# Two normed tiles of a fused transformer block: transposed by DMA and TensorE in halves, instead of by TensorE alone

## The chip, the cores and the metric

The kernel runs on one core of one Trainium2 chip. A core has five engines that matter here, each with an instruction order of its own: TensorE (PE, with its weight loads as PEld), VectorE (DVE), ScalarE (ACT), GpSimd (POOL) and SyncE (SP), which in this kernel issues nearly all DMAs. They meet only at semaphores: an instruction waits until the data that it reads are written and the buffer that it writes is free. The metric is the device time of one execution in microseconds (us); lower is better.

## The reference

The input is x, 2048 rows of 512 bf16 values, with a conditioning vector c. Cut to what matters:

```python
mod = (silu(c) @ w_mod).reshape(1, 6, 1, -1)         # sa, ca, ga, sb, cb, gb
h = layernorm(x) * (1 + ca) + sa                      # first norm
q, k, v = split(h @ wqkv)                             # 32 heads of 16
logits = q[s] . k[s - 2*w] / 4,  w = 0..7             # sliding, dilated window; masked below row 0
x = x + ga * ((softmax(logits) @ v) @ wo)
h = layernorm(x) * (1 + cb) + sb                      # second norm
x = x + gb * ((gelu(h @ w_gate) * (h @ w_up)) @ w_down)   # width 1792
```

Each row is normed twice. The normed rows then go into a product over the 512 columns, for which TensorE needs them with the columns on the partitions: each norm's output must be transposed.

## The kernel before, in words

**Tiling.** The 2048 rows are worked in 4 groups (sg 0 to 3) of 512 rows, each as 4 chunks (c4) of 128 rows, one row per partition. The 512 columns are 4 quarters (dt) of 128. LN1.1 means the first norm of group 1, LN2.0 the second norm of group 0, and so on.

**A norm.** For each chunk DVE takes the statistics (L430, L431; in some norms ACT does a chunk instead, L419); DVE adds the epsilon (L460, L465); GpSimd raises to the power -0.5 (`rs`, L471); DVE writes the normed chunk `xn` (L448, ops x0 to x3). The columns are then transposed, and at the same time or after it scaled by 1 + c and shifted by s, one quarter at a time (ops h0 to h3).

**Three ways to transpose.** `transp` (L475) and `transp_ev` (L514) hold two of them. By TensorE, for the norms in `BY_PE` (LN1.1 and LN2.0): two ops t0 and t1 of eight 128x128 transposes each, into PSUM (tile hTp, L484), then ACT evicts a quarter at a time with scale and shift (L527, 128x512). By DMA, for the norms of groups 1 to 3 otherwise: one transposing DMA on SP of all 16 blocks (L490), straight into the tile hT or h2, which ACT scales in place (L527), or GpSimd does for the norms in `H_POOL` (LN1.2; L525). LN1.0 has a way of its own by TensorE (`transp0`, `transp0_ev`, L509, L543, L545), which feeds the first products (L580).

**What uses them.** `qkv` (L588, products at L598) makes q (blk 0), k (blk 1) and v (blk 2) of a group, in four parts j; op qp.1.0.0 is the first product of group 1. Each takes four matmuls, one for each quarter. Loads for it are wqkv0 to wqkv2 (L223). `ffn_mm` (L826, products at L834) makes the gate and up products; g.0.0 is the first one of group 0.

**The attention** of a group: DVE multiplies q by the eight shifted k (`pq`, L659, op pq.sg.j), TensorE sums over a head with a 32-wide matrix of ones (`lp`, L673), DVE and ACT do the softmax (mx L690, z L696, e L701, s1 L706, ri L712, p L717). v goes to DRAM and back in shifted copies (`vst`, `V4`, L630, L639), the probabilities likewise (L745) or through TensorE, DVE multiplies them (`pv`, L766), TensorE sums (L780) and applies the output weights (`x1_mm`, L801), DVE adds the rest (L810).

**Order.** Every part is a generator ("thread") that yields `Op`s: engine, a cost, a function that issues the instructions, and what it waits for. `Issuer.run` (L94) takes the list `ORDER` (L19), a written-out list of thread numbers, and issues the next op of the thread named:

```python
for i in ORDER:
    op = nxt[i]
    assert all(name in self.done for name in op.after), (op.fire, op.after)
    ...
    op.fn()
```

So `ORDER` fixes the instruction order of every engine and of SP's DMA queue; `after`, `take` and `give` only state what must have been issued before. Nothing is reordered when the kernel runs.

Of the kernel before, what the change touches and what calls it, by code (L numbers as in the profile page):

```python
# [8 lines left out]
ACT = mybir.ActivationFunctionType  # L9
ALU = mybir.AluOpType  # L10
# [96 lines left out]
def kernel(  # L107
# [367 lines left out]
    def transp(key, dkey, dtag, ev):  # L475
        if ev in BY_PE:
            for dtp in range(2):
                def f(dtp=dtp):
                    hp = T("att", [P, CPS, 2, P], BF16, "hTp")
                    B[key, dtp] = hp  # L480
                    for c4 in range(CPS):
                        for dd in range(2):
                            dt = 2 * dtp + dd
                            nc.tensor.transpose(hp[:, c4, dd, :], B[key][:, c4, dt * P:(dt + 1) * P], ident[:])  # L484
                yield Op("PE", 0.445, f, after=[f"{ev}.x3", "ident"], take=[SL["att"]], give=[SL["xn"]] if dtp else [],
                         fire=f"{ev}.t{dtp}")
        else:
            def f():
                B[dkey] = T(dtag, [P, CPS, DT, P], BF16, dtag)
                nc.sync.dma_start_transpose(out=B[dkey][:].rearrange("p c d s -> p (c d) s"),  # L490
                                            in_=B[key][:].rearrange("p c d -> p (c d)"))
            yield Op("SP", 1.65, f, after=[f"{ev}.x3"], take=[SL[dtag]], give=[SL["xn"]], fire=f"{ev}.t", lat=1.0)
# [3 lines left out]
    BY_PE = ('LN1.1', 'LN2.0')  # L496
# [17 lines left out]
    def transp_ev(key, dkey, dtag, sc, bi, ev, dep):  # L514
        pe = ev in BY_PE
        for dtp in range(2):
            for dd in range(2):
                dt = 2 * dtp + dd

                def f(dt=dt, dtp=dtp, dd=dd):  # L520
                    if pe and dt == 0:
                        B[dkey] = T(dtag, [P, CPS, DT, P], BF16, dtag)
                    o = B[dkey][:, :, dt, :]
                    if ev in H_POOL:
                        nc.gpsimd.tensor_scalar(out=o, in0=o, scalar1=sc(dt), scalar2=bi(dt), op0=ALU.mult, op1=ALU.add)  # L525
# [26 lines left out]
    def ln1(sg):  # L552
        ev = f"LN1.{sg}"
        yield from norm(lambda: B["x", sg], lambda c4: [f"x0.{c4 // 2 * 2}"] if sg == 0 else [f"x{sg}"], ev,
                        PARTS0 if sg == 0 else ((0, 4),))
# [3 lines left out]
    def ln1_x(sg):  # L559
        yield from norm_x(("xn1", sg), lambda: B["x", sg], f"LN1.{sg}", PARTS0 if sg == 0 else ((0, 4),))  # L560

    def ln1_ev(sg):
        yield from transp_ev(("xn1", sg), ("hT", sg), "hT", lambda d: mod01[:, 4 + d:5 + d], lambda d: mod01[:, d:d + 1],
                             f"LN1.{sg}", ["mod01"])

# [22 lines left out]
    def qkv(sg):  # L588
        if sg == 0:
            yield from qkv_halves()  # L590
        for n, (blk, j) in enumerate(QKV if sg else QKV0):
# [10 lines left out]
            yield Op("PE", 0.865, f, after=[f"LN1.{sg}.h{d}" for d in (("0.1", "1.0", "3.1") if sg == 0 else (2, 3))] + [f"wqkv{blk}"], take=[SL["mm"]] + tk,  # L602
# [326 lines left out]
    for sg in range(NSG):  # L929
        for n, g in (("sa1", lambda q: norm_act(lambda: B["x", q], lambda c4: [f"x{q}"] if q else ["x0.2", "x0.0"], f"LN1.{q}")),  # L930
                     ("sa2", lambda q: norm_act(lambda: B["x", q], lambda c4: [f"x1.{q}.{c4}"], f"LN2.{q}")), ("ln1", ln1), ("ln1x", ln1_x), ("t1", lambda q: transp(("xn1", q), ("hT", q), "hT", f"LN1.{q}") if q else transp0(("xn1", 0), "LN1.0")), ("h1", lambda q: ln1_ev(q) if q else ln1_ev0(False)), ("qkv", qkv),
# [36 lines left out]
```

## Time and profile before

| What | Value |
|---|---|
| median of 3 runs | 237.67 us (237.32 to 238.6) |
| the profiled execution | 237.21 us |
| its span, first to last instruction | 235.0 us |
| granted TensorE clock in it | 1.0 |
| TensorE busy | 230.8 us |
| DVE busy | 170.1 us |
| ACT busy | 150.9 us |
| GpSimd busy | 17.9 us |

How to read it: the span is one execution as the hardware profiler recorded it; about 2 us lie outside it. Starts are in us from the start of the span. A row of the timeline has start, duration, engine, line, operation, output<-inputs, shapes and the count of instructions that it joins; matmuls overlap, so a row's duration is longer than the time it takes from the next. In brackets stands the idle time ahead of it and what ended that. The chain of work that ended last is followed back from the last instruction, at each step to what released it. Rows of DMA issues give the time from issue to landing as their last number.

### The profile page before, as it was taken

The numbers are of one execution on the slowest core, as the hardware profiler recorded it, in microseconds if no ns is written. First come the engines' busy times: TensorE is split into PE (matmuls) and PEld (weight loads), VectorE is DVE, ScalarE is ACT, GpSimd is POOL, SyncE is SP. The second block draws the span as 40 slices with busy tenths as digits, with TensorE's granted clock in tenths as the row PEclk, the third lists the DMA queues.
The fourth block names the chain that finished last, engine by engine and source line by source line (L and its number), as shares of the span: only waits on it lengthen the run. The fifth ranks groups of instructions, "written<-read, shape, count | busy, mean of one in ns | idle before, by whom it ended". The sixth has DMA issues, their size and how long they took to land.

```text
span 235.0 us, 3679 instructions
## 1 busy us (share of the span) xinstructions
PE 230.8 (98%) x1387; PEld 108.4 (46%) x1387; DVE 170.1 (72%) x238; ACT 150.9 (64%) x286; POOL 17.9 (8%) x43
## 2 busy tenths in 40 slices
PE   7999999999999999999999999999999999999995
PEld 2656454444644444444444444444444444444443
DVE  3899999999969999999899899279296211322222
ACT  4899997887996659937647862447636733367400
POOL 2612351000100000100000010000001000000000
PEclk9999999999999999999999999999999999999999
DMA  6998999999975859753100895320002210000011
GB/s 213 374 267 277 214 207 177 246 307 360 199 184 157 295 149 208 121 113 100 59 0 4 157 196 99 120 62 0 0 3 40 50 45 22 25 0 0 0 47 45
DMA packets 36265, 30.21 MB, mean 129 GB/s; under 512 B 14872, under 2 KB 34328, under 8 KB 36248
## 3 DMA queue, kind: packets, MB, share of 16 engines
q1 hardware_dynamic: 35968, 29.72, 50.7%
q8 instruction: 11, 0.18, 0.3%
q10 hardware_dynamic: 280, 0.26, 0.3%
q14 instruction: 6, 0.05, 0.1%
HBM read 22.37 MB, written 4.98 MB: 116 GB/s over the span
## 4 chain that ended last, share of the span: by engine, by line
PE 96%; ACT 2%; DVE 0%; issue 0%
PE u_ps L834 21%; PE g_ps L834 21%; PE y_ps L846 19%; PE qkv_ps L598 16%; PE x_ps L801 6%; PE LTp L673 3%; PE o_ps L780 3%; PE warm_ps L217 3%; PE y_ps L858 1%; PE hTp L484 1%; PE qkv_ps L580 1%; ACT hT L545 1%; ACT gl L419 1%; ACT LTp L701 0%; PE modT_ps L305 0%; PE modT_ps L348 0%
## 5 line engine op out<-in xcount | busy, mean ns | idle before, releaser
L834 PE MATMUL g_ps<-h,Wg 128*128 128x512 bf16 x224 | 57.5, 379 | 0.0
L834 PE MATMUL u_ps<-h,Wu 128*128 128x512 bf16 x224 | 57.5, 379 | 0.0
L868 ACT ACTIVATE gl<-g_ps 128x512 bf16<-128x512 f32 x56 | 33.5, 599 | 25.4 <-PE g_ps L834 22.1
L875 ACT CAST ub<-u_ps 128x512 bf16<-128x512 f32 x56 | 32.8, 586 | 21.4 <-PE u_ps L834 21.3
L846 PE MATMUL y_ps<-Wd,hht 128*128 128x512 bf16 x210 | 46.3, 379 | 0.0
L598 PE MATMUL qkv_ps<-hT,wqkv 128*128 128x512 bf16 x184 | 41.8, 380 | 0.1
L886 DVE TENSOR_TENSOR hht<-gl,ub 128x512 bf16<-128x512 bf16 x56 | 22.6, 420 | 25.2 <-ACT ub L875 23.2
L659 DVE TENSOR_TENSOR pq<-qT,kT 128x4096 bf16<-128x4096 bf16 x16 | 36.2, 2284 | 0.3 <-PE o_ps L780 0.2
L766 DVE TENSOR_TENSOR pv<-PT,V 128x4096 bf16<-128x4096 bf16 x16 | 35.9, 2283 | 0.0
L834 PEld LDWEIGHTS <-Wu 128*128 128x128 bf16 x224 | 21.6, 98 | 27.2 <-issue 1.9
L834 PEld LDWEIGHTS <-Wg 128*128 128x128 bf16 x224 | 21.6, 98 | 27.1 <-issue 1.7
L846 PEld LDWEIGHTS <-hht 128*128 128x128 bf16 x210 | 20.6, 98 | 24.8
L598 PEld LDWEIGHTS <-wqkv 128*128 128x128 bf16 x184 | 20.3, 114 | 19.6 <-issue 2.3
L893 DVE TENSOR_TENSOR ot<-y_ps,x 128x512 bf16<-128x512 f32 x15 | 10.3, 688 | 22.9 <-PE y_ps L846 22.9
L471 POOL TENSOR_TENSOR rstd<-rstd,neghalf 128x4 f32<-128x4 f32 (+1 forms) x9 | 8.9, 990 | 151.0 <-DVE rstd L460 81.3
L801 PE MATMUL x_ps<-woP,oT 128*128 128x512 bf16 x64 | 15.1, 379 | 0.0
L430 DVE BATCH_NORM_STATS2 st<-x 128x6 f32<-128x512 bf16 x18 | 12.3, 685 | 3.2 <-DMA x<-in_A_x_dram 2.9
L810 DVE TENSOR_TENSOR x<-x_ps,x 128x512 bf16<-128x512 f32 x16 | 10.8, 678 | 3.6 <-PE x_ps L801 3.4
L527 ACT ACTIVATE h<-h,modT,scl 128x512 bf16<-128x512 bf16 x12 | 8.8, 803 | 6.8 <-DMA h<-xn 6.8
L791 ACT CAST oT<-o_ps 128x512 bf16<-128x512 f32 x16 | 9.1, 590 | 3.5 <-PE o_ps L780 3.5
L620 ACT CAST kT<-qkv_ps 128x512 bf16<-128x512 f32 x16 | 9.6, 599 | 1.5 <-PE qkv_ps L598 1.4
L801 PEld LDWEIGHTS <-oT 128*128 128x128 bf16 x64 | 6.9, 109 | 7.1 <-issue 0.4
(84 smaller groups left out, 184.8 us busy)
## 6 DMA issues: line engine op xcount, KB each, us to landing
V<-vscr SPq DMA_DIRECT2D x12, 520.0 KB, 9.4
wm<-in_w_mod_dram SPq DMA_DIRECT2D x6, 512.0 KB, 5.9
vscr<-vT SPq DMA_DIRECT2D x4, 512.0 KB, 4.5
out_dram<-ot SPq DMA_DIRECT2D x15, 128.0 KB, 1.7
Wg<-in_B_w_gate_dram SPq DMA_DIRECT2D x1, 1792.0 KB
Wu<-in_B_w_up_dram SPq DMA_DIRECT2D x1, 1792.0 KB, 18.4
wqkv<-in_A_wqkv_dram SPq DMA_DIRECT2D x3, 512.0 KB, 8.5
x<-in_A_x_dram SPq DMA_DIRECT2D x3, 512.0 KB, 7.6
```

Source lines behind the costliest of these rows:

```text
L430: nc.vector.bn_stats(out=st[:], in_=src()[:, c4, :])
L598: nc.tensor.matmul(ps[:], lhsT=wqkv[blk][:, dt, j::4], rhs=B["hT", sg][:, :, dt, :], start=(dt == 0), stop=(dt == DT - 1))
L659: nc.vector.tensor_tensor(out=pq[:], in0=_ap(B["qT", sg][:, j, :], [[0, W], [1, SG]]), in1=_ap(kT[:, j, sg * SG + 2:sg * SG + 2 + SG], [[2 ...
L766: nc.vector.tensor_tensor(out=t[:], in0=_ap(B["PT", sg][:, 0, :], [[SG, 2], [0, 4], [1, SG]]), in1=_ap(v[:, 0, j, :], [[8, 2], [4 * (SG + ...
L801: nc.tensor.matmul(ps[:], lhsT=B["oT", sg][:, j, c4::CPS] if sg else B["oT", sg][:, j, c4 * P:(c4 + 1) * P], rhs=woP[:, j, :], start=(j == ...
L810: nc.vector.tensor_tensor(out=x[:, c4, :], in0=B["x1ps", sg, c4][:], in1=x[:, c4, :], op=ALU.add)
L834: nc.tensor.matmul(ps[:], lhsT=Wt[:, dt, ft * P:(ft + 1) * P], rhs=B["h2T", sg][:, :, dt, :], start=(dt == 0), stop=(dt == DT - 1))
L846: nc.tensor.matmul(ps[:], lhsT=B["hh", sg, ft][:, c4 * P:(c4 + 1) * P], rhs=B["Wd", ft // 4][:, ft % 4, :], start=(ft == 0), stop=(ft == F ...
L868: nc.scalar.activation(out=gl[:], in_=B["g", sg, ft][:], func=ACT.Gelu_apprx_tanh)
L875: nc.scalar.copy(out=ub[:], in_=B["u", sg, ft][:])
L886: nc.vector.tensor_tensor(out=hh[:], in0=B["gl", sg, ft][:], in1=B["ub", sg, ft][:], op=ALU.mult)
L893: nc.vector.tensor_tensor(out=ot[:], in0=B["y", sg, c4][:], in1=B["x", sg][:, c4, :], op=ALU.add)
```

## The change

For LN1.1 and LN2.0 the tile is transposed in two halves. `BY_PE` is emptied and a new `HALF` names the two norms.

- The first two chunks: as soon as x1 is written, one transposing DMA on SP moves their 8 blocks into the tile hT or h2. GpSimd scales and shifts them in place, a quarter at a time (ops hp0 to hp3, 128x256), in new threads.
- The last two chunks: one op t1 of 8 transposes on TensorE into PSUM, and four evictions of 128x256 on ACT (h0 to h3). These wait for the DMA too.
- The statistics of both norms are closed in two parts (`PARTS0`): two small steps on DVE and two powers on GpSimd (rs0, rs2) instead of one each.
- `qkv` of group 1 and `ffn_mm` of group 0 also wait for hp3.
- `ORDER` is a new list throughout.

In the new order, on SP: x1, x2, wqkv1, wqkv2, x3, wo0, LN1.1's transpose, wm2, wm3, the other wo blocks; and later V4.1.0, LN2.0's transpose, V4.1.1, V4.1.2 (before: x1, wqkv1, x2, and V4.1.0 to V4.1.2 in one piece). On GpSimd: rs0 and rs2 of LN1.1, hp0, rs0 of LN1.2, hp1, hp2, hp3; and rs0, rs2, hp0 to hp3 of LN2.0. On DVE around LN2.0: the last statistics, x0, x1, the softmax's z, x2, x3, s1, ri, p, then pq.2.0 and pq.2.1 in a row.

```diff
 ORDER = [
...
+        elif ev in HALF:
+            def f():
+                B[dkey] = T(dtag, [P, CPS, DT, P], BF16, dtag)
+                nc.sync.dma_start_transpose(out=B[dkey][:, 0:2].rearrange("p c d s -> p (c d) s"),
+                                            in_=B[key][:, 0:2].rearrange("p c d -> p (c d)"))
+            yield Op("SP", 1.65, f, after=[f"{ev}.x1"], take=[SL[dtag]], fire=f"{ev}.t", lat=0.5)
+
+            def f():
+                B[key, 0] = T("att", [P, DT, 2, P], BF16, "hTp")
+                for dt in range(DT):
+                    for c4 in range(2):
+                        nc.tensor.transpose(B[key, 0][:, dt, c4, :], B[key][:, 2 + c4, dt * P:(dt + 1) * P], ident[:])
+            yield Op("PE", 0.445, f, after=[f"{ev}.x3", "ident"], take=[SL["att"]], give=[SL["xn"]], fire=f"{ev}.t1")
...
-    BY_PE = ('LN1.1', 'LN2.0')
+    BY_PE = ()
+
+    HALF = ('LN1.1', 'LN2.0')
+
+    HALF_POOL = ('LN1.1', 'LN2.0')
...
     def transp_ev(key, dkey, dtag, sc, bi, ev, dep):
         pe = ev in BY_PE
+        if ev in HALF:
+            for dt in range(DT):
+                def f(dt=dt):
+                    nc.scalar.activation(out=B[dkey][:, 2:4, dt, :], in_=B[key, 0][:, dt, :, :], func=ACT.Identity,
+                                         scale=sc(dt), bias=bi(dt))
+                yield Op("ACT", 0.455, f, after=[f"{ev}.t1", f"{ev}.t"] + dep, give=[SL["att"]] if dt == DT - 1 else [],
+                         fire=f"{ev}.h{dt}")
+            return
...
+    def half_ev(dkey, sc, bi, ev, dep):
+        for dt in range(DT):
+            def f(dt=dt):
+                o = B[dkey][:, 0:2, dt, :]
+                if ev in HALF_POOL:
+                    nc.gpsimd.tensor_scalar(out=o, in0=o, scalar1=sc(dt), scalar2=bi(dt), op0=ALU.mult, op1=ALU.add)
...
+            yield Op("POOL" if ev in HALF_POOL else "ACT", 0.44 if ev in HALF_POOL else 0.47, f, after=[f"{ev}.t"] + dep,
+                     fire=f"{ev}.hp{dt}")
...
-        yield from norm(lambda: B["x", sg], lambda c4: [f"x1.{sg}.{c4}"], ev)
+        yield from norm(lambda: B["x", sg], lambda c4: [f"x1.{sg}.{c4}"], ev, PARTS0 if ev in HALF else ((0, 4),))
...
-        h2 = [f"LN2.{sg}.h3"]
+        h2 = [f"LN2.{sg}.h3"] + ([f"LN2.{sg}.hp3"] if f"LN2.{sg}" in HALF else [])
```

More of the change, by code (lines that the diff above doesn't have):

```diff
@@ L531, in transp_ev @@
                          give=[SL["att"]] if pe and dd == 1 else [], fire=f"{ev}.h{dt}")
+    def half_ev(dkey, sc, bi, ev, dep):
[4 more added lines that the diff above has]
+                    nc.gpsimd.tensor_scalar(out=o, in0=o, scalar1=sc(dt), scalar2=bi(dt), op0=ALU.mult, op1=ALU.add)
+                else:
+                    nc.scalar.activation(out=o, in_=o, func=ACT.Identity, scale=sc(dt), bias=bi(dt))
+            yield Op("POOL" if ev in HALF_POOL else "ACT", 0.44 if ev in HALF_POOL else 0.47, f, after=[f"{ev}.t"] + dep,
+                     fire=f"{ev}.hp{dt}")
     def transp0_ev(key, dkey, sc, bi, ev, dep, eng):
@@ L554, in ln1 @@
         yield from norm(lambda: B["x", sg], lambda c4: [f"x0.{c4 // 2 * 2}"] if sg == 0 else [f"x{sg}"], ev,
-                        PARTS0 if sg == 0 else ((0, 4),))
+                        PARTS0 if sg == 0 or f"LN1.{sg}" in HALF else ((0, 4),))
     PARTS0 = ((0, 2), (2, 4))
     def ln1_x(sg):
-        yield from norm_x(("xn1", sg), lambda: B["x", sg], f"LN1.{sg}", PARTS0 if sg == 0 else ((0, 4),))
+        yield from norm_x(("xn1", sg), lambda: B["x", sg], f"LN1.{sg}", PARTS0 if sg == 0 or f"LN1.{sg}" in HALF else ((0, 4),))
     def ln1_ev(sg):
@@ L564, in ln1_ev, with ln1_evh @@
                              f"LN1.{sg}", ["mod01"])
+    def ln1_evh(sg):
+        yield from half_ev(("hT", sg), lambda d: mod01[:, 4 + d:5 + d], lambda d: mod01[:, d:d + 1], f"LN1.{sg}", ["mod01"])
     def ln1_ev0(onv):
@@ L601, in qkv @@
             tk = {0: [SL["q"]], 1: [], 2: [SL["vs"]]}[blk] if j == 0 else []
-            yield Op("PE", 0.865, f, after=[f"LN1.{sg}.h{d}" for d in (("0.1", "1.0", "3.1") if sg == 0 else (2, 3))] + [f"wqkv{blk}"], take=[SL["mm"]] + tk,
+            yield Op("PE", 0.865, f, after=[f"LN1.{sg}.h{d}" for d in (("0.1", "1.0", "3.1") if sg == 0 else (2, 3))] + ([f"LN1.{sg}.hp3"] if f"LN1.{sg}" in HALF else []) + [f"wqkv{blk}"], take=[SL["mm"]] + tk,
                      give=[SL["hT"]] if last else [], fire=f"qp.{sg}.{blk}.{j}")
@@ L814, in ln2 @@
         ev = f"LN2.{sg}"
-        yield from norm(lambda: B["x", sg], lambda c4: [f"x1.{sg}.{c4}"], ev)
+        yield from norm(lambda: B["x", sg], lambda c4: [f"x1.{sg}.{c4}"], ev, PARTS0 if ev in HALF else ((0, 4),))
     def ln2_x(sg):
-        yield from norm_x(("xn2", sg), lambda: B["x", sg], f"LN2.{sg}")
+        yield from norm_x(("xn2", sg), lambda: B["x", sg], f"LN2.{sg}", PARTS0 if f"LN2.{sg}" in HALF else ((0, 4),))
     def ln2_ev(sg):
@@ L822, in ln2_ev, with ln2_evh @@
                              lambda d: modT[:, d:d + 1], f"LN2.{sg}", ["mod3", "mod4"])
+    def ln2_evh(sg):
+        yield from half_ev(("h2T", sg), lambda d: scl[:, d:d + 1], lambda d: modT[:, d:d + 1], f"LN2.{sg}", ["mod3", "mod4"])
     LAST = ((0, 384), (384, 512))
     def ffn_mm(sg):
-        h2 = [f"LN2.{sg}.h3"]
+        h2 = [f"LN2.{sg}.h3"] + ([f"LN2.{sg}.hp3"] if f"LN2.{sg}" in HALF else [])
         for ft in range(FT):
@@ L930 @@
         for n, g in (("sa1", lambda q: norm_act(lambda: B["x", q], lambda c4: [f"x{q}"] if q else ["x0.2", "x0.0"], f"LN1.{q}")),
[L931 removed]
+                     ("sa2", lambda q: norm_act(lambda: B["x", q], lambda c4: [f"x1.{q}.{c4}"], f"LN2.{q}")), ("ln1", ln1), ("ln1x", ln1_x), ("t1", lambda q: transp(("xn1", q), ("hT", q), "hT", f"LN1.{q}") if q else transp0(("xn1", 0), "LN1.0")), ("h1", lambda q: ln1_ev(q) if q else ln1_ev0(False)), ("h1h", lambda q: ln1_evh(q) if f"LN1.{q}" in HALF else iter(())), ("h2h", lambda q: ln2_evh(q) if f"LN2.{q}" in HALF else iter(())), ("ln2a", lambda q: rst(f"LN2.{q}", 0, 2, []) if f"LN2.{q}" in HALF else iter(())), ("qkv", qkv),
                      ("qev", qkv_ev), ("v", vload), ("pq", logits), ("lmm", logits_mm), ("soft", soft), ("ptd", lambda q: pt_dma(q) if q in PT_DMA else iter(())), ("pv", pv), ("pvmm", pv_mm), ("pvev", pv_ev), ("x1mm", x1_mm),
```

71 rows, old and new, of the table ORDER are left out of this document.

## The prediction

> **What bounds the kernel now.** I read four views: the page (busy shares and the chain that ended last), the chain in order of time, the rows of TensorE around both norms, and the queues that feed them.
>
> The page:
> ```profile
> span 235.0 us, 3679 instructions
> PE 230.8 (98%) x1387; PEld 108.4 (46%) x1387; DVE 170.1 (72%) x238; ACT 150.9 (64%) x286; POOL 17.9 (8%) x43
> PEclk9999999999999999999999999999999999999999
> PE 96%; ACT 2%; DVE 0%; issue 0%
> ```
> TensorE is busy for 98% of the span, at full granted clock, and makes 96% of the chain. What leaves TensorE shortens the run by its own length; each wait put on TensorE lengthens it. The profiled execution took 237.21 for its span of 235.0; the median of the runs is 237.67, 0.46 above it. I add the sum to 237.67.
>
> The transposes in question, from the view of the tile hTp (ns: lowest, median, highest), then the chain in order of time:
> ```profile
> L484 PE MATMUL hTp<-ident,xn x32: 216/219/219, 20.3 to 64.0; 128*128 128x128 bf16 x32
> L545 ACT ACTIVATE hT<-hTp,mod x3: 557/562/564, 9.2 to 10.1; 128x256 bf16<-128x256 bf16 x3
> ...
> 20.50 0.89 PE hTp L484 x16
> 28.34 0.98 PE LTp L673 x16
> 40.57 0.86 PE LTp L673 x16
> ```
> Sixteen transposes cost TensorE 0.89; the 219 ns each overlap. The two LTp rows are the same work: 0.98 where it stands between 128-wide products, 0.86 where it follows other 32-wide ones. So a switch between the two kinds costs about 0.12.
>
> TensorE's rows around both changes:
> ```profile
> 10.33 0.27 PE L580 MATMUL qkv_ps<-hT,wqkv 128*128 128x256 bf16 x1
> 10.76 1.80 PE L580 MATMUL qkv_ps<-hT,wqkv 128*128 128x256 bf16 x15 [0.16 <-ACT hT L545]
> 12.39 8.10 PE L598 MATMUL qkv_ps<-hT,wqkv 128*128 128x512 bf16 x36
> 23.01 0.40 PE L369 MATMUL gR_ps<-wm,scB 128*32 128x128 bf16 x16
> 23.28 0.61 PE L673 MATMUL LTp<-pq,Mph 128*32 128x512 bf16 x8
> 23.83 0.41 PE L598 MATMUL qkv_ps<-hT,wqkv 128*128 128x512 bf16 x1
> ...
> 64.10 1.89 PE L598 MATMUL qkv_ps<-hT,wqkv 128*128 128x512 bf16 x8
> 65.82 1.03 PE L834 MATMUL g_ps<-h,Wg 128*128 128x512 bf16 x4
> ```
> A product of four takes 1.03 alone and 1.89 in a pair, so they run 0.86 apart. Group 1's first product is at 23.83, group 0's first gate product at 65.82; these use what the change produces. TensorE runs up to both without a break, so there is no slack on it.
>
> **The change, part by part.**
>
> *Transposes.* 16 of 32 leave TensorE: 0.89, on the path: **-0.89**. ACT's evictions become 128x256 (562 ns by the row above); their length matters only where named below.
>
> *The start.* A matmul stood at 10.33 and the next at 10.76, waiting for ACT's hT. The first matmul goes on at 0.11 steps (1.80 for 15), so 0.32 is lost. The new order has the first transposes earlier and gives this buffer sooner: **-0.32**, bounds -0.32 and 0.
>
> *The second weight block.* On SP the new order issues the load of x2 ahead of wqkv1, where it was x1, wqkv1, x2. The SP rows of before, and the load view (us to landing):
> ```profile
> 2.91 0.53 SPq L231 DMA_DIRECT2D x<-in_A_x_dram  x1
> 3.48 0.44 SPq L223 DMA_DIRECT2D wqkv<-in_A_wqkv_dram  x1
> 13.99 0.35 SPq L231 DMA_DIRECT2D x<-in_A_x_dram  x1
> ...
> x<-in_A_x_dram SPq DMA_DIRECT2D x1, 512.0 KB, 7.6
> wqkv<-in_A_wqkv_dram SPq DMA_DIRECT2D x1, 512.0 KB, 8.5
> ```
> x1 landed at 2.91 + 7.6 = 10.51, wqkv1 at 3.48 + 8.5 = 11.98: 1.47 apart. Moved one place back, wqkv1 lands at 13.45; the load of 13.99, which waited its turn behind these, gives the late end. TensorE wants it one product after 12.39: 12.39 + 0.86 - 0.32 = 12.93. That is a wait of 0.5 to 1.06: **+0.8**. Nothing else can run meanwhile, since TensorE's order is fixed.
>
> *Switches.* TensorE has two more changes between 128-wide and 32-wide work: 2 x 0.12 = **+0.24** (0 to 0.24).
>
> *Group 1.* The DVE rows of xn and of one statistics step, the landing times of the full transposes and of the wm blocks, SP's transposing row, and GpSimd's rows:
> ```profile
> 18.20 1.05 DVE L448 TENSOR_SCALAR xn<-x,mv,rstd 128x512 bf16<-128x512 bf16 x3
> ...
> 58.56 0.69 DVE L430 BATCH_NORM_STATS2 st<-x 128x6 f32<-128x512 bf16 x1
> 59.29 0.18 DVE L431 BATCH_NORM_AGGREGATE mv<-st 128x2 f32<-128x6 f32 x1
> ...
> 61.52 0.73 DVE L448 TENSOR_SCALAR xn<-x,mv,rstd 128x512 bf16<-128x512 bf16 x2
> ```
> ```profile
> h<-xn SPq DMA_TRANSPOSE x1, 4.7
> ...
> h<-xn SPq DMA_TRANSPOSE x1, 4.3
> ...
> wm<-in_w_mod_dram SPq DMA_DIRECT2D x6, 512.0 KB, 5.9
> ```
> ```profile
> 22.29 3.04 SPq L490 DMA_TRANSPOSE hT<-xn  x1
> ...
> 18.37 1.25 POOL L471 TENSOR_TENSOR rstd<-rstd,neghalf 128x4 f32<-128x4 f32 x1 [3.15 <-DVE rstd L465]
> 27.48 5.26 POOL L525 TENSOR_SCALAR hT<-hT,mod 128x512 bf16<-128x512 bf16 x4 [7.87 <-PE qkv_ps L598]
> ...
> L525 POOL TENSOR_SCALAR hT<-hT,mod x4: 768/769/3002, 27.5 to 32.0; 128x512 bf16<-128x512 bf16 x4
> ```
> LN1.1's first two chunks are ready about 15.0: x1 landed at 10.51, then come four statistics of 0.87 (one of them LN1.2's) and two xn in 0.73, with the pow beside the statistics. Half the blocks land 2.2 (half of 4.3) to 4.7 after issue: by 19.7. One hp of 128x256 is between 0.385 (half of 0.769) and 0.769; I take 0.45, near the half. hp0 then ends at 20.2, rs0 of LN1.2, now queued behind it on GpSimd, at 21.4, hp3 at 22.8. TensorE is at group 1's first product at about 23.3 (23.83 + 0.48 from the start, less 0.44 of transposes and 0.55 for a logits step now behind it) and wants the last quarter 0.65 later: 1.2 to spare. On SP the loads of wm2 and wm3 move behind this transpose (about 1.5, half of 3.04): issued by 17.0, landed 5.9 later by 22.9. The gR product, which uses wm2 and stood at 23.01, now comes at about 21.8, so it waits 0 to 1.1. The queue is nearly empty by then, so I take **+0.3** for these and for small waits on evictions (0 to 1.3).
>
> Without group 0's second norm, that is -0.89 - 0.32 + 0.8 + 0.24 + 0.3 = **+0.13**.
>
> *Group 0's second norm.* The two scaled chunks are ready about 60.4: statistics to 59.47, one small step of 0.17, two xn in 0.73, which now stand ahead of the softmax's subtraction. But on SP this transpose is behind the first V4 load of group 1. SP and its landing times:
> ```profile
> 44.85 0.97 SPq L223 DMA_DIRECT2D Wu<-in_B_w_up_dram  x1
> 50.63 4.01 SPq L639 DMA_DIRECT2D V<-vscr  x3
> ...
> Wu<-in_B_w_up_dram SPq DMA_DIRECT2D x1, 1792.0 KB, 18.4
> ```
> ```profile
> V<-vscr SPq DMA_DIRECT2D x1, 520.0 KB, 15.1
> ```
> Wu landed at 44.85 + 18.4 = 63.2, V at 50.63 + 15.1 = 65.7. A transpose behind them lands at 65.7 or after: I take 66.5, bounds 62.6 (60.4 + 2.2, as if alone) and 68. Now DVE and GpSimd:
> ```profile
> 25.35 4.48 DVE L659 TENSOR_TENSOR pq<-qT,kT 128x4096 bf16<-128x4096 bf16 x2
> ...
> 65.55 2.28 DVE L659 TENSOR_TENSOR pq<-qT,kT 128x4096 bf16<-128x4096 bf16 x1
> ```
> One of GpSimd's four scalings above took 3.00 instead of 0.77, and it began at 27.48, just before a pq (DVE's 25.35 row is two of them, the second from about 27.56 to 29.84): GpSimd stood until that pq ended. In the new order pq.2.0 and pq.2.1 are back to back. They start at 65.55 + 0.46 (shift so far: -0.32 + 0.8 + 0.3 - 0.44 + 0.12) + 0.17 for one more small DVE step = 66.2. The transpose lands at 66.5, so all four hp wait until 66.2 + 4.48 = 70.7 and end at 70.7 + 4 x 0.45 = 72.5. TensorE reaches g.0.0 at 65.82 + 0.13 and its last quarter at 66.6. The stall is 72.5 - 66.6 = **+5.9**. Nothing behind g.0.0 can pass it.
>
> [...]
>
> Sum: +0.13 + 5.9 = +6.0, **243.7** on the median. Own range: 242.6 (hp at 0.385, wqkv1 at 13.45, no small waits in group 1) to 245.6 (hp at 0.769, wqkv1 at 13.99).
>
> **Rivals.**
>
> *GpSimd is held less.* The transpose lands before pq.2.0, or the four hp get in after one pq. For: the landing's bounds include 65.7; only one of four scalings was held in before. Against: pq.2.0 and pq.2.1 follow with nothing between. At best ACT sets the end: its four evictions write the same tile and wait for the transpose too, 65.7 + 4 x 0.562 = 67.9, a stall of 1.3. With one pq: 66.2 + 2.28 + 1.8 = 70.3, a stall of 3.7. With +0.13 that is 239.1 to 241.5.
>
> *Not slower.* It all hangs on the landing: if the transpose passes the V load and lands by 64.5 (60.4 + 4.1, as the idle queue gave 4.3 for twice the blocks), the hp end before pq.2.0 and ACT ends at 66.7. Then only +0.13 stays, 237.8; with wqkv1 in time, -0.7, 237.0. For: V's bytes and the transposes need not share the slowest engine. Against: 18.4 and 15.1 us to landing.
>
> *Group 1 is starved too.* If the xn of LN1.2, which run with hp1 to hp3, hold GpSimd as pq does, hp3 waits for pq.0.1 to pq.0.3, about 29.9, for a product at 24.0: +6 more, 249.7. Against: the pow at 18.37 ran beside such xn and took 1.25, not several us. [...]
>
> *Faster by more than 0.5%.* That needs -1.2, so every gain and none of the losses (-0.89 - 0.32 = -1.21).
>
> **How the numbers follow.** 0.5%, or 1.2 us, is about what a measurement of this kernel can tell from no change. Forecast 0.50, GpSimd held less 0.25, not slower 0.15, group 1 starved 0.05, faster 0.05. Slower is 0.50 + 0.25 + 0.05 = 0.80, same 0.15, faster 0.05. The range for 8 in 10 takes in the first three cases, less some edge: 237.4 to 245.6. The forecast with "held less" has 0.75, from 239.1.
>
> **What would show it.** Sixteen transposes in the tile view, eight per norm. A gap of 0.5 to 1.06 on TensorE at 12.9 to 14, ended by the wqkv load. No gap at 10.3. No gap above 0.3 ahead of group 1's first product near 23.3; if one of 6 is there, the third rival holds. A gap of about 5.9 ahead of or inside the first gate product, ended by GpSimd's scaling, with the four hp after 70.7 and the transpose landing near 66.5. [...] What else could spoil it: the landing time on a queue whose order is new throughout, which no row of before shows.

## The result, and the profile after

The changed kernel takes 240.73 us (median; 239.85 to 247.12) against 237.67 before: 1.0112 times as long, with a 95% interval of 1.0077 to 1.0147. Timed again beside the experiments it took 240.1 (239.59 to 242.04) against 237.81, ratio 1.0107 (1.0055 to 1.0160). It is slower, as forecast, and inside the range, but by 2.7 (1.12% of 237.67) instead of 6.0. Its executions fall into two groups: of the eleven timed or profiled, nine lie between 239.6 and 242.0 and two at 247.1 and 247.9; the ratios are of the first group, and both are shown below, since they differ above all in one place of the program.

The page of an execution of the first group (240.39 us):

```profile
span 238.6 us, 3648 instructions
PE 229.9 (96%) x1359; PEld 107.5 (45%) x1371; DVE 170.7 (72%) x239; ACT 149.8 (63%) x286; POOL 24.6 (10%) x53
```

Its transposes for the two norms, in the view of the tile hTp, are 16 where they were 32:

```profile
L499 PE MATMUL hTp<-ident,xn x16: 219/219/219, 20.6 to 65.3; 128*128 128x128 bf16 x16
```

So TensorE has 0.9 less to do, by the forecast's 0.89 for 16, and the span is 3.6 longer: about 4.5 are lost elsewhere. (The 1359 matmuls of this page lack 12 records: there are 1371, 16 fewer than before. So its busy time is a little too low.) What TensorE waited for (us in total, times, longest) in that execution, and then in the kernel before:

```profile
PE g_ps L877 <- DVE ot L936: 1.4, 1, 1.4
PE LTp L713 <- DVE pq L699: 1.3, 1, 1.3
PE warm_ps L218 <- DVE gB L213: 1.2, 1, 1.2
PE PTp L771 <- DVE e L757: 0.6, 1, 0.6
PE hTp L527 <- DVE xn L449: 0.4, 1, 0.4
PE qkv_ps L638 <- DMA wqkv<-in_A_wqkv_dram: 0.3, 1, 0.3
```

```profile
PE warm_ps L217 <- DVE gB L212: 1.2, 1, 1.2
PE qkv_ps L580 <- ACT hT L545: 0.2, 1, 0.2
```

Three of the new waits are for VectorE's pq, probabilities (e) and output steps (ot), and one is for a load. (The 0.4 for xn stands at the start, between warm-up products: TensorE came to its first 128x512 product at 12.36, and at 12.39 before.) None is at the second norm. The rows of TensorE give their places:

```profile
13.66 2.56 PE L638 MATMUL qkv_ps<-hT,wqkv 128*128 128x512 bf16 x11 [0.28 <-DMA wqkv<-in_A_wqkv_dram]
...
25.49 0.62 PE L713 MATMUL LTp<-pq,Mph 128*32 128x512 bf16 x8 [1.25 <-DVE pq L699]
...
40.03 0.62 PE L771 MATMUL PTp<-e,ident 128*32 128x256 bf16 x16 [0.61 <-DVE e L757]
...
67.98 1.03 PE L877 MATMUL g_ps<-h,Wg 128*128 128x512 bf16 x4
...
116.56 1.02 PE L877 MATMUL g_ps<-h,Wg 128*128 128x512 bf16 x4 [1.42 <-DVE ot L936]
```

The four brackets make 3.56. A stop costs about 0.17 on top of its bracket, by the forecast's row (a product takes 1.03 alone and 0.86 in a row), so the four cost about 4.2 of the 4.5; this is an estimate. The first gate product of group 0, at 67.98, waits for nothing. In an execution of the second group (247.12 us) the same product stood still:

```profile
72.88 0.38 PE L877 MATMUL g_ps<-h,Wg 128*128 128x512 bf16 x1 [4.44 <-POOL h L564]
73.42 0.40 PE L877 MATMUL g_ps<-h,Wg 128*128 128x512 bf16 x1 [0.16 <-POOL h L564]
73.64 1.89 PE L877 MATMUL u_ps<-h,Wu 128*128 128x512 bf16 x4
75.32 1.89 PE L877 MATMUL g_ps<-h,Wg 128*128 128x512 bf16 x4
77.03 1.04 PE L877 MATMUL u_ps<-h,Wu 128*128 128x512 bf16 x4
```

GpSimd's and VectorE's rows there, in the long execution and then in the short one (L564 is the in-place scaling hp0 to hp3, L699 is pq):

```profile
66.92 6.45 POOL L564 TENSOR_SCALAR h<-h,scl,modT 128x256 bf16<-128x256 bf16 x4 [3.75 <-ACT h L537]
...
68.00 4.48 DVE L699 TENSOR_TENSOR pq<-qT,kT 128x4096 bf16<-128x4096 bf16 x2
```

```profile
65.94 2.16 POOL L564 TENSOR_SCALAR h<-h,scl,modT 128x256 bf16<-128x256 bf16 x4 [2.42 <-ACT qT L658]
...
68.34 4.49 DVE L699 TENSOR_TENSOR pq<-qT,kT 128x4096 bf16<-128x4096 bf16 x2
```

Four scalings take 2.16 when nothing is in the way. In the short execution they start 2.40 ahead of pq.2.0 and are done. In the long one they start 1.08 ahead, two get through, and the other two wait until both pq have ended at 72.48. The third's own record runs from 68.00 to 72.83: it had been started and stood at its work, not at a semaphore. So semaphores are not the only place where two engines of this kernel meet.

### The profile page after: what moved, and what is told of

The parts are those of the page before. It is cut to its first block, busy times and chain, and to the rows that moved or that the text cites. A ratio compares the mean times of both kernels' runs of the same rounds, so it can differ in the third digit from the quotient of the medians.

```text
span 245.1 us, 3660 instructions
## 1 busy us (share of the span) xinstructions
PE 232.7 (95%) x1371; PEld 107.8 (44%) x1371; DVE 171.2 (70%) x239; ACT 150.3 (61%) x286; POOL 28.4 (12%) x53
## 4 chain that ended last, share of the span: by engine, by line
PE 68%; DVE 10%; DMA 8%; ACT 6%; POOL 4%; issue 2%; SPq 1%; POOLq 0%; ACTq 0%
PE u_ps L877 18%; PE g_ps L877 18%; PE y_ps L889 14%; PE x_ps L841 6%; PE qkv_ps L638 6%; DVE pq L699 4%; DMA x<-in_A_x_dram 3%; PE o_ps L820 3%; DMA V<-vscr 3%; POOL h L564 3%; ACT gl L420 2%; PE LTp L713 2%; DVE xn L449 1%; DMA hT<-xn 1%; PE y_ps L901 1%
## 5 line engine op out<-in xcount | busy, mean ns | idle before, releaser
L877 PE MATMUL g_ps<-h,Wg 128*128 128x512 bf16 x224 | 58.9, 384 | 6.1 <-POOL h L564 4.6
L877 PE MATMUL u_ps<-h,Wu 128*128 128x512 bf16 x224 | 58.4, 384 | 0.0
L929 DVE TENSOR_TENSOR hht<-gl,ub 128x512 bf16<-128x512 bf16 x56 | 22.8, 421 | 33.5 <-ACT ub L918 33.3
L699 DVE TENSOR_TENSOR pq<-qT,kT 128x4096 bf16<-128x4096 bf16 x16 | 36.0, 2283 | 0.0
L472 POOL TENSOR_TENSOR rstd<-rstd,neghalf 128x2 f32<-128x2 f32 (+1 forms) x11 | 9.4, 854 | 145.2 <-DVE rstd L466 61.7
L658 ACT CAST qT<-qkv_ps 128x512 bf16<-128x512 f32 x16 | 9.5, 598 | 2.4 <-PE qkv_ps L638 2.4
L409 ACT ACTIVATE gl<-x 128x512 bf16<-128x512 bf16 x14 | 8.9, 640 | 2.7 <-DVE x L850 2.0
## 6 DMA issues: line engine op xcount, KB each, us to landing
Wg<-in_B_w_gate_dram SPq DMA_DIRECT2D x1, 1792.0 KB, 17.9
```

Source lines behind the costliest of these rows:

```text
L699: nc.vector.tensor_tensor(out=pq[:], in0=_ap(B["qT", sg][:, j, :], [[0, W], [1, SG]]), in1=_ap(kT[:, j, sg * SG + 2:sg * SG + 2 + SG], [[2 ...
L877: nc.tensor.matmul(ps[:], lhsT=Wt[:, dt, ft * P:(ft + 1) * P], rhs=B["h2T", sg][:, :, dt, :], start=(dt == 0), stop=(dt == DT - 1))
L929: nc.vector.tensor_tensor(out=hh[:], in0=B["gl", sg, ft][:], in1=B["ub", sg, ft][:], op=ALU.mult)
```

## The experiments

In all of them only the order of instructions, the engine of a scaling or the way of a transpose changes; a move is written below as the order on one engine. The changed kernel's code is meant unless the kernel before is named.

### The race at the second norm

The changed kernel again; LN2.0's scaling on ScalarE; LN2.0's transposing DMA two places later:

> The changed kernel once more, for a second profile. Port theory (GpSimd's four scalings of the second norm race pq.2.0 for VectorE's and GpSimd's common way to SBUF): times fall near 240 when all four are done before pq.2.0 starts, and near 247 when one is caught (it then waits for two pq, 4.5, and TensorE idles 4.6). In a profile near 240 scaling hp3 ends before pq.2.0 starts and the gap in the first gate product is under 1.5. Rival (the time is lost at the start and in the small waits alone, and a slower clock makes the long runs): the scalings stand in the same way in short and long runs.

> The changed kernel with the second norm's in-place scaling (hp0 to hp3 of LN2.0) on ScalarE behind h3, in place of GpSimd. Port theory: no time near 247 any more, since ScalarE does not stand while pq runs; ScalarE adds 4 x 0.58 = 2.3 behind h3 (67.4), so the last quarter is ready near 69.7 against 68.3: about 1.4 later than the changed kernel's short runs, 241 to 242. Rival (a slower clock makes the long runs): times near 247 stay about as frequent.

```diff
-    HALF_POOL = ('LN1.1', 'LN2.0')
+    HALF_POOL = ('LN1.1',)
 ScalarE:
-h0 h1 h2 h3 | next evictions
+h0 h1 h2 h3 | hp0 hp1 hp2 hp3 | next evictions
```

> The changed kernel with LN2.0's transposing DMA issued behind V4.1.1 and V4.1.2 instead of ahead of them. Port theory: it lands after pq.2.0 has started, so all four scalings wait until pq.2.1 has ended near 72.5 and end near 74.7: every run is long, 247 to 249, with a gap of 6 in the first gate product and no short run. Rival (GpSimd gets a turn between the two pq): the scalings run from 70.3 and the gap is 3 to 4, 244.

```diff
 SyncE:
-V4.1.0, LN2.0.t, V4.1.1, V4.1.2
+V4.1.0, V4.1.1, V4.1.2, LN2.0.t
```

Measured: again 240.1, with the short profile above. On ScalarE 241.89 (241.57 to 242.32), none of four runs long (which alone says little, at two in eleven). With the later DMA 248.18 (247.2 to 250.62), every run long:

```profile
71.39 3.40 POOL L564 TENSOR_SCALAR h<-h,scl,modT 128x256 bf16<-128x256 bf16 x4 [7.96 <-issue]
...
68.25 4.48 DVE L699 TENSOR_TENSOR pq<-qT,kT 128x4096 bf16<-128x4096 bf16 x2
```

The port theory holds in all three in what it says of the times: with a later landing alone, all four runs are long, with a gap of 5.2 for the 6 expected. A slower clock is not the cause: in the long execution the granted clock is 1.0 through the stop of 4.44 and 0.5 only behind it, from 73.64 (last section). What these runs show is that the one stands while the other works (the third scaling from 68.00 to 72.83, beside pq.2.0 and pq.2.1); that the two engines have a way to SBUF in common was the author's assumption, which no trace or run here shows. With the later DMA the landing itself was late (71.39), so that run does not tell whether GpSimd could have had a turn between the two pq; the long execution above tells that: its third scaling, caught at 68.00, got none. The kernel before had shown the same: its first scaling began at 27.48, while one pq ran (25.35 to 27.63), and stood through the next, to 29.84; it took 3.00, the other three 0.77 each. In none of the profiles was a scaling that came ready inside a pq done before the last of the back-to-back pq had ended.

The later experiments gave more profiles of the same race. The start of hp0 against the start of pq.2.0:

| Profile | Transpose issued | hp0 starts | pq.2.0 starts | ahead by | caught |
|---|---|---|---|---|---|
| changed, long | 62.34 | 66.92 | 68.00 | 1.08 | yes |
| changed, short | 62.69 | 65.94 | 68.34 | 2.40 | no |
| wqkv1 first (below) | 62.90 | 67.48 | 68.55 | 1.07 | yes |
| rs0 first (below) | 61.42 | 64.70 | 67.06 | 2.36 | no |
| ot first (below) | 62.21 | 65.48 | 67.86 | 2.38 | no |
| rs0 and ot first (below) | 61.65 | 65.72 | 67.30 | 1.58 | yes |

The dividing line lies between 1.58 and 2.36, where four scalings (2.16) put it. pq.2.0 starts 5.6 to 5.7 after the transpose's issue in all six; hp0, which waits for the landing, starts 3.2 to 4.6 after it. So it is the landing that moves.

One try to make the margin larger, two scalings on ScalarE:

> The changed kernel with hp2 and hp3 of LN2.0 on ScalarE behind h3, hp0 and hp1 left on GpSimd. Port theory: two scalings on GpSimd end 1.1 after the landing (66 to 67), before pq.2.0 starts at 68.0 to 68.4, so no run is long; ScalarE's two add 1.2 behind h3 (67.4), 68.6 against 68.3: 240.1 to 240.6, highest under 243. Rival (long runs come from the clock): some of the runs are near 247.

```diff
+    def on_pool(ev, dt):
+        return ev in HALF_POOL and (ev != 'LN2.0' or dt < 2)
```

(hp2 and hp3 then follow h3 on ScalarE.) 240.36 (239.97 to 241.74), no long run in eight, as expected. That did not settle it: a later kernel with the same split (a_back, below) was caught all the same in one profile, because the transpose had landed 5.4 after its issue:

```profile
66.92 5.24 POOL L567 TENSOR_SCALAR h<-h,scl,modT 128x256 bf16<-128x256 bf16 x2 [4.59 <-ACT h L537]
...
67.15 4.66 DVE L702 TENSOR_TENSOR pq<-qT,kT 128x4096 bf16<-128x4096 bf16 x2
```

hp0 was under way when pq.2.0 started, and the two pq took 4.66 for 4.48; hp1 stood until both were done. So the split makes the race rarer, not safe: over all kernels with it 2 of 48 runs were long, over those with four scalings on GpSimd and the transpose at its place 5 of 30.

### What makes the short executions slower

The load order at the start:

> The changed kernel with the load of wqkv1 issued ahead of x2 again, as before the change. If the wait for wqkv1 (1.15 in the profile of the changed kernel, 12.73 to 14.09) is on the path and nothing takes its place: 0.9 to 1.2 shorter than the changed kernel, about 239. If the statistics of group 1 and 2 then come late in its place (x2 lands one place later): within 0.3 of the changed kernel.

```diff
 SyncE:
-x1, x2, wqkv1, wqkv2
+x1, wqkv1, x2, wqkv2
```

240.62 (240.42 to 247.23): nothing gained. In its profile (of the long execution) TensorE no longer waits for wqkv1, but 0.8 for the wm3 load and 0.5 for pq.0.1 at the next places: other waits took its place.

Why pq.0.1 is late, in the short profile of the changed kernel (GpSimd, then VectorE):

```profile
19.56 0.56 POOL L564 TENSOR_SCALAR hT<-hT,mod 128x256 bf16<-128x256 bf16 x1 [3.36 <-DMA hT<-xn]
20.08 1.01 POOL L472 TENSOR_TENSOR rstd<-rstd,neghalf 128x4 f32<-128x4 f32 x1
21.08 1.69 POOL L564 TENSOR_SCALAR hT<-hT,mod 128x256 bf16<-128x256 bf16 x3
```

```profile
18.80 0.41 DVE L449 TENSOR_SCALAR xn<-x,sums,rstd 128x512 bf16<-128x512 bf16 x1
21.12 1.23 DVE L449 TENSOR_SCALAR xn<-x,mv,rstd 128x512 bf16<-128x512 bf16 x2 [1.92 <-POOL rstd L472]
22.28 0.96 DVE L449 TENSOR_SCALAR xn<-x,sums,rstd 128x512 bf16<-128x512 bf16 x2
23.16 8.88 DVE L699 TENSOR_TENSOR pq<-qT,kT 128x4096 bf16<-128x4096 bf16 x4
```

hp0 waits for the DMA; rs0 of LN1.2 stands behind it on GpSimd; VectorE's next four instructions need rs0, and it idles 1.92. The kernel before started the same pq at 20.95, this one at 23.16. One instruction moved, on GpSimd; one on VectorE; and both:

> The changed kernel with one instruction moved on GpSimd: rs0 of LN1.2 ahead of hp0 of LN1.1. Queue theory: hp0 waits for the transposing DMA until 19.6, rs0 behind it ends at 21.1, and VectorE, which has nothing else in its order, idles from 19.4 to 21.1; so everything of VectorE up to 60 is about 2 late, and TensorE waits for it (lp.0.1 for pq.0.1 1.4, the probabilities of group 0 0.8, lp.1 0.3). With rs0 first the xn start at 19.9, these waits fall by 1.2 to 2 in all: 238.1 to 238.9. If an hp is then caught by pq.0.1, a gap of 5 ahead of group 1's first product, 243 or more. Rival (VectorE's own new order makes it late): within 0.4 of the changed kernel's 240.1.

```diff
 GpSimd:
-LN1.1.hp0, LN1.2.rs0, LN1.1.hp1
+LN1.2.rs0, LN1.1.hp0, LN1.1.hp1
```

> The changed kernel with one instruction moved on VectorE: the output step ot.0.2 ahead of pq.3.2 instead of behind it. In the changed kernel TensorE waits 1.58 near 115 in group 1's first products, for ot.0.2 to free a PSUM buffer. If that wait is on the path and nothing takes its place: 238.5 to 238.9. Rival (VectorE is late anyway, and lp.3.2 or the products of pv wait in its place): within 0.4 of 240.1.

```diff
 VectorE:
-ot.0.0, ot.0.1, pq.3.2, ot.0.2
+ot.0.0, ot.0.1, ot.0.2, pq.3.2
```

> Both of the moves, rs0 of LN1.2 ahead of hp0 and ot.0.2 ahead of pq.3.2. If the two losses are independent, the two gains add: 240.1 - 1.5 - 1.5 = 237.1 (236.4 to 237.6), at or under the kernel before. If they share a cause (a late VectorE), the second adds under 0.5 to the first: 238.5.

Measured: rs0 first 239.43 (239.02 to 245.66), ratio to before 1.0063 (1.0046 to 1.0080). The idle time is 0.58, pq.0.1 starts at 21.90, and TensorE's wait for it is gone from the view:

```profile
18.47 1.10 POOL L472 TENSOR_TENSOR rstd<-rstd,neghalf 128x4 f32<-128x4 f32 x1 [2.44 <-DVE rstd L466]
19.57 2.26 POOL L564 TENSOR_SCALAR hT<-hT,mod 128x256 bf16<-128x256 bf16 x4
...
19.61 1.23 DVE L449 TENSOR_SCALAR xn<-x,mv,rstd 128x512 bf16<-128x512 bf16 x2 [0.58 <-POOL rstd L472]
...
21.90 8.88 DVE L699 TENSOR_TENSOR pq<-qT,kT 128x4096 bf16<-128x4096 bf16 x4
```

The queue theory (rs0 behind the waiting hp0 makes VectorE late) holds, with half or less of the 1.2 to 2 hoped for: 240.1 - 239.43 = 0.7. That the wait is gone is plain; the 0.7 is a difference of medians, and the intervals of the two ratios overlap, here and in the next two runs. ot first 239.41 (238.79 to 239.68), 0.7 gained of 1.5: TensorE's wait for ot fell from 1.4 to 0.6, since ot.0.2 then waits 1.30 for an output buffer, until a store of ot has landed. Both 238.97 (238.47 to 244.93), ratio 1.0049 (1.0031 to 1.0067): the gains do not add in full.

Then the order alone, with all 32 transposes on TensorE:

> The new order alone: all 32 transposes on TensorE and whole-tile evictions on ScalarE as before the change, statistics closed in one part, no in-place scaling, but every other instruction in the changed kernel's order. Queue theory: no hp0 ahead of rs0 of LN1.2, so the wait of lp.0.1 falls under 0.3; 0.89 of transposes comes back, the waits for wqkv1 and at 115 stay: 238.8 to 239.8, and no long run. Rival (the new order itself is the loss): lp.0.1 waits 1 or more as in the changed kernel, 240.5 to 241.

```diff
 the kernel before, all engines:
-the old order
+the new order (t0, t1 where it has t1; no transposing DMA and no scaling in place for LN1.1 and LN2.0)
```

The statistics are closed in one part here, so LN1.1's x0 and x1 come later than in the changed kernel. Measured: 240.83 (240.53 to 240.99), ratio 1.0130 (1.0113 to 1.0147), no run long. Its waits:

```profile
PE g_ps L834 <- DVE ot L893: 1.4, 1, 1.4
PE warm_ps L217 <- DVE gB L212: 1.2, 1, 1.2
PE PTp L731 <- DVE e L717: 0.5, 1, 0.5
PE qkv_ps L598 <- DMA wqkv<-in_A_wqkv_dram: 0.4, 1, 0.4
```

The queue theory is right that the wait for pq.0.1 goes, but the time came out as the rival had it. The new order costs 3.0 with no half transposed by DMA. The halves themselves, in this order, gain 0.1 to 0.7 by the medians (240.73 and 240.1 for the changed kernel); the intervals overlap.

With the first norm in halves and the second by TensorE as before the change:

> The changed kernel with LN2.0 transposed by TensorE alone as before the change, LN1.1 in halves. 8 transposes come back: 0.44, so 240.4 to 240.8 if the second norm's half costs nothing in the short runs, and no run near 247, since GpSimd has nothing left to scale there. Rival (the second norm's half costs something in short runs too): 239.6 to 240.2.

```diff
-    BY_PE = ()
-    HALF = ('LN1.1', 'LN2.0')
+    BY_PE = ('LN2.0',)
+    HALF = ('LN1.1',)
```

240.95 (240.63 to 242.53), no long run. Beside the order alone, 240.83, the first norm's half gains nothing: 0.44 of transposes against the wait behind hp0 (0.5 for pq.0.1 in its profile). By these medians, what the halves gain in short executions is the second norm's, but the intervals overlap (1.0118 to 1.0170 here). It is the second norm's half that makes the long executions profiled.

### Which places of the new order

First an attempt to undo the places inside the changed kernel:

> The split scaling, rs0 of LN1.2 ahead of hp0, and two orders put back near where they were before the change: on VectorE the outputs ot.0.0 to ot.0.2 ahead of the pq they stood behind (with their stores), on TensorE the transposition of group 0's probabilities two products later and lp.1.2 two products later. If the new order is the loss and these are its places: rs0 -0.7, ot -1.5, probabilities and lp.1.2 -0.8, so 237.0 to 237.6, at the kernel before. If a late VectorE passes the waits on to the next reader instead: 238.3 to 238.9.

(The split scaling and rs0 first are as above; the rest is)

```diff
 VectorE:
-s1.2, ri.2, p.2, pq.3.0, pq.3.1, ot.0.0, ot.0.1, pq.3.2, ot.0.2
+ot.0.0, s1.2, ri.2, p.2, ot.0.1, pq.3.0, ot.0.2, pq.3.1, pq.3.2
 TensorE:
-ptp.0, qp.2.2.1, qp.2.2.2 ... lp.1.1, lp.1.2, qp.2.0.1, qp.2.1.1
+qp.2.2.1, qp.2.2.2, ptp.0 ... lp.1.1, qp.2.0.1, qp.2.1.1, lp.1.2
```

> The same, and at the start wqkv1 ahead of x2 on SyncE, lp.0.1 one product later and the product of wm3 two products later on TensorE. If the wait for wqkv1 (0.4 to 1.15 in the profiles) is then on the path with nothing in its place: 0.4 to 0.9 under the run without it, 236.3 to 237.2, faster than the kernel before. If another wait takes its place, as it did when wqkv1 alone was moved: within 0.3 of the run without it.

240.26 (239.93 to 248.22) and 241.32 (240.58 to 242.25): both lie outside both of their expectations. The waits for ot and for the probabilities are gone, and another stands in their place, for a logits step that the new order has early and this kernel left there:

```profile
PE LTp L716 <- DVE pq L702: 1.5, 1, 1.5
PE warm_ps L218 <- DVE gB L213: 1.2, 1, 1.2
PE qkv_ps L641 <- DMA wqkv<-in_A_wqkv_dram: 0.5, 1, 0.5
PE o_ps L823 <- DVE pv L809: 0.4, 1, 0.4
```

The first one's long run has no profile; which scaling was caught is open. So the places were put, one at a time, into the kernel before:

> The kernel before the change, with one DMA moved: the load of x2 issued ahead of wqkv1, as in the changed kernel. TensorE is packed there, so a wait of 0.5 to 1.06 at the first key product is on the path: 238.3 to 238.8. Rival (it is taken up by VectorE's lateness behind it): within 0.3 of 237.8.

```diff
 SyncE:
-x1, wqkv1, x2
+x1, x2, wqkv1
```

> The kernel before the change, with the changed kernel's order on TensorE around 38 to 45 alone: the transposition of group 0's probabilities two products earlier, the logits step lp.1.2 right behind lp.1.1. If the waits of 0.8 and 0.3 there come from this order: 237.8 + 0.8 to 1.4 = 238.6 to 239.2. Rival (VectorE's lateness from group 1's norm makes them): within 0.4 of 237.8.

```diff
 TensorE:
-qp.2.2.1, qp.2.2.2, ptp.0, lp.1.0, lp.1.1, qp.2.2.3 ... qp.2.0.3, lp.1.2
+ptp.0, qp.2.2.1, qp.2.2.2, qp.2.2.3, lp.1.0, lp.1.1, lp.1.2 ... qp.2.0.3
```

> The kernel before the change, with the changed kernel's order around 110 to 116 alone: on VectorE pq.3.0, pq.3.1, ot.0.0, ot.0.1, pq.3.2, ot.0.2, hh.1.0, ot.0.3, on TensorE lp.3.0 and lp.3.1 ahead of g.1.0, the stores as there. If the wait of 1.6 for ot at 115 comes from this order: 237.8 + 1.4 to 2.0 = 239.2 to 239.8. Rival (it needs a VectorE that is late for other reasons): within 0.4 of 237.8.

```diff
 VectorE:
-ot.0.0, s1.2, ri.2, p.2, ot.0.1, pq.3.0, ot.0.2, pq.3.1, ot.0.3, hh.1.0, pq.3.2
+s1.2, ri.2, p.2, pq.3.0, pq.3.1, ot.0.0, ot.0.1, pq.3.2, ot.0.2, hh.1.0, ot.0.3
 TensorE:
-y.0.3.1, g.1.0 ... g.1.4, lp.3.0, lp.3.1
+y.0.3.1, lp.3.0, lp.3.1, g.1.0 ... g.1.4
```

> The kernel before the change with three pieces of the new order together: x2 ahead of wqkv1, the probabilities and lp.1.2, and the ot. If the new order's loss (3.0 in the run of the order alone) is these three places: 240.0 to 241. If waits share slack, less than the sum of the three single runs; if other places of the order matter, the sum is well under 3.0.

(ScalarE's copies of the probabilities and SyncE's stores move along with these.)

| Kernel before, with | Time | Kernel before beside it | Difference | Ratio (95%) |
|---|---|---|---|---|
| x2 ahead of wqkv1 | 238.30 | 237.82 | +0.48 | 1.0006 to 1.0033 |
| probabilities two products earlier, lp.1.2 earlier | 239.20 | 237.65 | +1.55 | 1.0046 to 1.0084 |
| two logits steps ahead of g.1.0, pq ahead of ot | 239.52 | 237.65 | +1.87 | 1.0059 to 1.0094 |
| all three | 241.34 | 237.65 | +3.69 | 1.0134 to 1.0174 |

```profile
40.60 0.62 PE L731 MATMUL PTp<-e,ident 128*32 128x256 bf16 x16 [1.32 <-DVE e L717]
```

This row, of the second kernel, shows its wait for the probabilities. But its profile has another wait, and so has the third kernel's:

```profile
PE qkv_ps L598 <- DMA wqkv<-in_A_wqkv_dram: 1.0, 1, 1.0
```

```profile
PE qkv_ps L598 <- DMA wqkv<-in_A_wqkv_dram: 1.0, 1, 1.0
PE u_ps L834 <- DVE ot L893: 0.6, 1, 0.6
PE o_ps L780 <- DVE pv L766: 0.3, 1, 0.3
```

This 1.0 is for the third weight block, at 17.9 and 17.7. Neither edit touches its load, and the one profile of the kernel before has no such wait. So a part of the +1.55 and of the +1.87 may be that load's and not the place's; no run here tells how much. The profile of all three together is free of it: its waits at the three places are 0.8 for wqkv1, 1.3 for the probabilities, 0.6 for ot and 0.3 for pv, which is 3.0 of its 3.69. So together the three places are enough for the 3.0 of the order alone; that the single losses, 3.90, come out near the 3.69 of all three does not show that they add. The order also gives something back, as the wait at 10.76 that is gone.

Last, the undoing done in full: from group 2's softmax sum on, every instruction in the old order, the probabilities later, rs0 first, the scaling split:

> The changed kernel with the places of its order undone more fully: from the softmax sum of group 2 (s1.2, about 104) on, every instruction in the order of before the change; the probabilities of group 0 and lp.1.2 two products later, qp.2.0.3 ahead of o.0.0; rs0 of LN1.2 ahead of hp0. The scaling is split: hp3 of LN1.1, hp2 and hp3 of LN2.0 on ScalarE. wqkv1 stays behind x2. If those places made the loss: 240.1 - 1.6 - 0.9 - 0.7 = 236.9, with the waits of the split 236.9 to 238.0, level with the kernel before or under it, and no long run. If a late VectorE passes the waits on again, as in a_fix: 239 to 240.

```diff
 GpSimd:
-LN1.1.hp0, LN1.2.rs0, LN1.1.hp1, hp2, hp3
+LN1.2.rs0, LN1.1.hp0, hp1, hp2            (hp3 on ScalarE)
 TensorE:
-ptp.0, qp.2.2.1, qp.2.2.2 ... lp.1.2, qp.2.0.1, qp.2.1.1 ... o.0.0, o.0.1, qp.2.0.3
+qp.2.2.1, qp.2.2.2, ptp.0 ... qp.2.0.1, qp.2.1.1, lp.1.2 ... qp.2.0.3, o.0.0, o.0.1
 all engines from s1.2 on:
-the new order
+the old order
```

> The same with all four scalings of LN1.1 on GpSimd. If GpSimd's four end before pq.0.1 (2.26 from 19.6 to 21.9, pq.0.1 from 21.9): 0 to 0.3 under a_back, with a long run, near 245, where one is caught. If one is always caught: 243 or more.

238.46 (237.98 to 246.31) against 238.03, ratio 1.0014 (0.9991 to 1.0036); and 238.56 (238.17 to 239.93), ratio 1.0032 (1.0016 to 1.0048). The loss goes from 1.1% to 0.1% or 0.3%. So the order from s1.2 on, the place of the probabilities and rs0 carry nearly all of it inside the changed kernel as well. The first can't be told from the kernel before and still has a long run in thirteen; the second is slower by its 0.3%. No version here beat the kernel before.

## Why the prediction was right or wrong

Two terms of the sum failed: the +5.9 at group 0's second norm, which did not happen in nine of eleven executions, and the +0.13 for all the rest, which measured 2.7. That the result lies inside the range is luck, since the two errors go opposite ways.

*The sign* is right, though the loss forecast for it is not the one that came. *The transposes, -0.89:* there are 16 in the tile view. The order alone, with 32, is slower by only 0.1 to 0.7, with overlapping intervals; the rest of the 0.89 would have gone into the wait behind hp0, so that its full worth is not shown. The switches' 0.24 was not measured by itself.

*The start, -0.32 and +0.8 for wqkv1:* right in both mechanisms. The wait for ScalarE's eviction is gone, and TensorE comes to its first 128x512 product at 12.36 in the short profile and 12.08 in the long one, for 12.39 before and 12.07 forecast; so the 0.32 holds in one of the two. It waits at the first key product (0.28 by the bracket of the short profile, 1.0 in the long one's view of waits; forecast 0.5 to 1.06). Moved alone into the kernel before, the load cost +0.48; undone in the changed kernel, it gave nothing, for other waits came in its place.

*Group 1, +0.3 (0 to 1.3), and with it "+0.13 without group 0's second norm":* this step failed. The chain hp0, rs0, hp3 was put against TensorE's first product of group 1, and for that it was right: hp3 ended at 22.77 (22.8 forecast). But rs0 has another reader, VectorE, and it was not followed there: 1.92 idle, 1.25 of it handed to TensorE at 25.49. And beyond the start and the two norms the forecast gave the new order nothing, without a reason. Two of its three costly places (40.03 and 116.56; 0.61 and 1.42) stand where the change itself does nothing. Without any stall at the second norm the loss was 2.7, not 0.13.

*Group 0's second norm, +5.9:* this step failed too. That a scaling stands behind pq was right (68.00 to 72.83); what was wrong is the landing's place against pq.2.0. In the long execution it went as written: hp caught at pq.2.0, free when pq.2.1 ends, 4.44 and 0.16 on TensorE. In nine of eleven it did not happen, as one term was mis-sized, the time from the transpose's issue to its landing: 6.1 in the forecast (60.4 to 66.5), 3.2 to 4.6 by hp0's start. VectorE was 2 late, and with it both the issue (62.3 to 62.7) and pq.2.0 (68.0 to 68.3, not 66.2); the landing did not move with them and came at 65.9 to 66.9, near the 66.5 forecast. So the forecast had it 0.3 behind pq.2.0's start; hp0 starts 1.1 to 2.4 ahead of it. That it would land behind the loads in front of it was right, as the last section shows. One scaling takes 0.54 to 0.56, between the bounds of 0.385 and 0.769.

*The rival "GpSimd is held less":* its time, 239.1 to 241.5, holds the result; its mechanism does not. It had a stall of 1.3 to 3.7 left at the second norm. There was none. *"Not slower"* had the four hp done before pq.2.0, as in nine of eleven, though by a landing at 64.5 and not by a late pq.2.0; it failed by the +0.13. *"Group 1 is starved too":* no. hp1 to hp3 ran beside the four xn at 0.56 each; the xn were stretched instead (two took 1.23 against 1.05 for three before).

*The own range* does not follow from the terms that it names: with the scaling at 0.385, the load's wait at 0.52 and no small waits the sum is 242.9, not 242.6, and at its other end 245.2, not 245.6. Nothing hangs on it.

## What to carry to other kernels

When an instruction that waits for a DMA is put into an engine's queue, list what stands behind it there and who reads that, on every engine, not only the reader that the change is about: here the power of another group's norm, and behind it VectorE. When an order is made anew, cost the whole of it, since the loss can lie far from the edit; running the new order with the old operations tells the two apart in one run. In these traces a GpSimd scaling beside back-to-back pq got through only if it had begun before the first of them; so here such work needed a gap on VectorE as long as the work itself (2.16 for four scalings: 2.36 was enough, 1.58 was not), plus the spread of the landing that it waits for (3.2 to 5.4 after the issue).

## What the runs showed that was not expected

The caught execution costs more than its stall. Behind the idle 4.44, eight matmuls (two products) run at half pace: rows 73.64 and 75.32 take 1.89 for four matmuls, 77.03 again 1.04, so 2 x 0.85 = 1.7 is lost on top. With the 4.44 and 0.16 that is 6.3 of the 6.5 by which the two spans differ (245.1 and 238.6). The granted clock of the long execution is 0.5 from 73.64 to 77.05, and 1.0 on both sides. So the half clock lasted 3.4 there, behind a stop of 4.44; the short execution, whose longest wait is 1.42, has a mean clock of 1.0. How long a stop brings the half clock on, and what ends it, was not shown.

The landing of one and the same transpose of 8 blocks, at the same place of the program, spread from 3.2 to 5.4 after its issue over the profiles (by the start of the scaling that waits for it). That spread decides between 240 and 247. The traces tell what it goes with, the load of Wg (the gate weights) in front of it on SP's queue. In the long execution and then in the short one, its issue and its time to landing, then the transpose's time to landing (its issue stands in the table of the race):

```profile
46.56 0.51 SPq L224 DMA_DIRECT2D Wg<-in_B_w_gate_dram  x1
Wg<-in_B_w_gate_dram SPq DMA_DIRECT2D x1, 1792.0 KB, 17.9
h<-xn SPq DMA_TRANSPOSE x1, 4.4
```

```profile
46.86 0.51 SPq L224 DMA_DIRECT2D Wg<-in_B_w_gate_dram  x1
Wg<-in_B_w_gate_dram SPq DMA_DIRECT2D x1, 1792.0 KB, 16.1
h<-xn SPq DMA_TRANSPOSE x1, 3.1
```

Wg landed at 64.4 and 63.0, the transpose at 66.8 and 65.8. In the twelve profiles with the transpose at this place it never landed sooner than 3.1 after its issue, nor sooner than 2.2 after Wg; in the eight where Wg landed more than 0.8 behind the transpose's issue, the transpose came 2.2 to 2.4 after Wg. This is read from the traces: no run moved the Wg load by itself, and what moves Wg's own landing (61.9 to 65.0) stays open.
